# Sliding-window attention and a gated feed-forward network: the RMS root from block 3 on as one GpSimd power, with re-laid orders

## The chip, the core and the metric

The kernel runs on one core of a Trainium2 chip. Its engines are TensorE (PE in the profile; PEld are its weight loads), VectorE (DVE), ScalarE (ACT), GpSimd (POOL) and SyncE (SP). Each works through its own queue in order, and they meet at semaphores. GpSimd and SyncE also issue transfers (DMAs). The metric is the time of one execution on the device, in microseconds (us). Before the change it is 241.68 us, the median of three runs from 241.58 to 241.69.

## What is computed

Attention with a window of 128 keys and 4 sink keys, over 4 batches, 8 heads, 768 positions and head size 64; its output, read as 3072 tokens of 512 numbers, goes through an RMS norm and a gated network of inner size 1536.

```python
def _attn_ref(q, k, v, n_sink, window):
    scores = scale * np.matmul(q, k.transpose(0, 1, 3, 2))
    keep = is_sink | in_window
    scores = np.where(keep, scores, -1000000000.0)
    a = np.exp(scores - np.max(scores, axis=-1, keepdims=True))
    a = a / (np.sum(a, axis=-1, keepdims=True) + 1e-09)
    return np.matmul(a, v)

def _moe_ref(x, w_gate, w_val, w_out, rms_g):
    rms = np.sqrt(np.mean(x * x, axis=-1, keepdims=True) + 1e-06)
    xn = x / rms * rms_g
    g = xn @ w_gate
    silu = g * (1.0 / (1.0 + np.exp(-g)))
    return silu * (xn @ w_val) @ w_out
```

## The kernel before

**Blocks and groups.** The tokens are cut into 24 blocks of 128, numbered g = 0 to 23, six to a batch. Four blocks form a group G = 0 to 5 of the network, 512 tokens wide. Attention of a block needs its own keys and values, those of the block before, and the four sinks. Block g's keys are also met by the queries of block g + 1, so its scores need q of g and g + 1.

**One block's way.** Its q, k and v are loaded in bf16 by GpSimd (`load_bf16`, `load_v`; the transfer converts). q and k are transposed: for g under 8 by TensorE (`pe_t`), with a copy out of the bank by ScalarE or VectorE (`copy_t`, written kT and qT below); from 8 on by a transposing transfer on SyncE's queue (`dma_t`, L459). TensorE makes the scores s (L485, L501, L563), ScalarE their exponentials (L512, L536, L572), VectorE or, from block 16, GpSimd masks them (L547, L584; L526, L597). TensorE multiplies with v in two halves u (`av`, L616, L621), and VectorE divides by the sums (`normal`, n below: L660, L661). Then comes the norm: `square` (L669, ScalarE) sums the squares into `ms`; `rms` (VectorE) makes 1/root of it with six operations on 128 x 1 (L676 adds epsilon, L680 guesses by the number's bits, L689 four times refines) and scales x with it and with the row `gb` (L693, out xr; `gb` holds the norm's weight times the constant `C3` of the refinement). xr is transposed (xt), by TensorE and a copy for g under 8, and by SyncE (`dma_x`, L720) from 8 on.

**The network.** Per group, projections g and v of 12 feature tiles (L975; `ffn`, `mms`), tanh (L982), two VectorE products (L988, p1; L998, h) and the output product (L1008, three parts for each block of 128 tokens), evacuation (L1016, osb) and store (L1020, st). Group 0 is worked in quarters of 128 tokens, groups 1 and 2 in halves, the rest whole.

**The order.** It is written out by hand. Every piece of work is an operation of `plan`, with the ways it can be done, a cost in ns, what it needs and gives, and the PSUM banks it takes and drops. The table `ORDER` lists for each engine the numbers of its operations in order, `TURNS` the sequence in which the engines' lists are taken, `BANKS` the bank for each taking. `Plan.run` follows them, and asserts that all needs have been given. So an engine's queue holds its operations exactly as `ORDER` has them; semaphores come from the data alone. A need such as `("s", g - LOAD_LEAD)` on a load makes no semaphore; it only bounds where the load may stand in the list.

**Names for the lists.** Read with the operations' names, GpSimd's list has, from its 26th place on, and SyncE's from its 8th (q4 is the load of q of block 4; wo0 and wo6 the halves of the output weight; qT, kT, xt the transposes; st0.1 the store of group 0's block 1):

```
GpSimd  q4 v3 k4 q5 q6 wo0 k5 v4 wo6 q7 v8 q8 v5 k6 k7 k8 v6 v7 q9 k9 v9 q10 k10 v10 q11 k11 v11
        q12 k12 v12 ... (in the order of blocks) ... q20, then masks of blocks 16 and 17, k20, ...
SyncE   qT8 qT9 kT8 kT9 qT10 st0.0 qT11 kT10 kT11 qT12 qT13 kT12 kT13 qT14 st0.3 xt8 qT15 xt9 ...
```

Of the kernel before, what the change touches and what calls it, by code (L numbers as in the profile page):

```python
# [96 lines left out]
399 401 400 402 728 418 419 733 420 393 421 409 763 758 778 768 754 773 744 749 427 433
414 783 434-436 448 449 793 450 798 451 442 808 788 819 803 463-466 813 457 824 480 475
482 494 496 497 495 513 488 514 515 504 834 838 516 848 843 853 829 863 868 858 878 873
525 883 531-533 893 509 888 534 899 923 549-551 928 552 938 543 567-569 918 570 585 587  # L100
933 943 948 561 953 579 958 909 904 968 593 963 914 973 1008 1003 994 998 1013 1028 1023
989 1038 1018 1033 984 1053 1048 1043 979 1069 1059 1064 1072 1073
# [29 lines left out]
ASDDSDGDPDPSPDPPPPPGPPPGPDPGPPDDPGAGPPPPADGPPPPGPPSPDPSADPGSDPSPGAAAPAGPAPPDAPPGPPAPDPAP  # L132
PPPADPGPDAGPPDPPDGAPPGPAPPAGDPAPAPDGADAPDGPAPPPADPAGPDAPADAGPPPPAPADGAPADGPPPPPAPPDPGPPD
DPAGPDPAGPDPGAPDDGPDGPDADGDPDGPADADPGAADPGPGDPADGAPDPGADAPGADADPGDPAPPDAPPDADAPGDPPADAGP
AAGPAPDAPPDPADPDAPGDAPDDGDPAPGDPPGSAAPGADAPGDPDGPPPDAGDAPGDADPPGADPAGDSAPPAGASPADPADSADP
PPGADAPGPSADDPGASAPGDPGSAPPGDPSADGAPDASDAPPDADPAGPPSAAADPAADPADPDAPAGADPGADPPDAPPADDPDGS
PDAPASAGDPPAPAGDSPADAPADDPPAGSADPPDASDPAGPADPSDDPGAPDDPADAPDGSDPDGPAGAPADSAPPADSDPPDGPDS
PDAGASPAAPDASGDPADSPDSDPGSPPPDDPSDGPDADPAPADPSDPSPDPSPDDAPDPDAPADPADAPDADAPDPDPASAPDASAP
DSADPADPDPASAPASADPAPPDASDPDAPSDASPADPDADPDPDPDAPASAPPDASADPAGPDGPGDPDGAPDPDPDPDAPAAGPSA
DGPAASGPADSPAGDPPGDDPGPPDGPDAAGPPDAGADPAGPAAGDPADAGPGPDSPGDPDASGPDGAADSPDAPDSDPPDSPDAPDS  # L140
ADPDSAPPDSDPSDAPDASPADDPDPDPADAPAAPDASADPADSPGSDGPDGSPGPGPAPAPADPAPDADPADAPDAGAPDGPGPAAP
AAPPADGDPPDGPDGDGPPAAPDSPGDPGAGPDAPPDPDPDPDAADPADPDDPAPAADPSDPDPDDPAAPPSPDDPAAPDPPSPPDPA
PSDSDSPASDPDPPPAAPDDPDPDPPAAPSDPDPAPDDPDPPPPAAPDADPSDPAAPDPDPAAPDDPDPDAPADPDPDPDPPDPAAPD
# [997 lines left out]
```

## Time and profile before

| | |
|---|---|
| median of three runs | 241.68 us |
| span of the profiled execution, first to last instruction | 241.9 us |
| ScalarE busy | 122.8 us |
| GpSimd busy | 89.2 us |
| loads of q, k, v: issues by GpSimd | 70, 0.89 us each on the mean |

The profile is one execution, taken by the hardware. A row of a group has line, engine, operation, out<-in, count, then after the bar the busy time in us and the mean of one in ns, then the idle time just before and what ended it. A row of a timeline has start and length in us, engine, line, operation, out<-in, count, and in brackets the engine's idle time before it and what ended that. A row of the table by stretches has the stretch, its length, and each engine's busy time with its instructions in brackets (PE, PEld, DVE, ACT, POOL), then the granted clock of TensorE, the busy share of the transfers' engines and GB/s.

### The profile page before, as it was taken

Reading aid. Unit: us, or ns where it says so; the run is one execution under the profiler, and the core shown is the slowest. Engines: PE = TensorE matmul, PEld = TensorE weight load, DVE = VectorE, ACT = ScalarE, POOL = GpSimd, SP = SyncE. Lnnn points to the kernel's source line nnn. Section 1 sums busy time; section 2 is a strip of 40 time slices with the busy share of each in tenths; the row PEclk is TensorE's granted clock in tenths of the full one; section 3 lists DMA queues with packets and bytes.
Section 4 is the critical chain, followed back from the end, with each engine's and each line's share of the span. In section 5 each row is a group of like instructions: output and inputs, shape, how many; then the busy total and the mean of one; then the engine's idle time right before and its main releaser. Section 6 shows DMA issues by size and latency. Waiting matters only on the chain.

```text
span 241.9 us, 5897 instructions
## 1 busy us (share of the span) xinstructions
PE 231.3 (96%) x2329; PEld 147.6 (61%) x2354; DVE 187.4 (77%) x478; ACT 122.8 (51%) x267; POOL 89.2 (37%) x116
## 2 busy tenths in 40 slices
PE   7889999999879999999999999999999999999995
PEld 5568986876668776777876644445554444444443
DVE  3599989989979999999898989994569946537520
ACT  4776368667766574337654464454543321233112
POOL 8985894597526554000004982022540000000000
PEclk9999999999999999999999999999999999999999
DMA  9999999999999999999601999527010114101024
GB/s 128 143 183 195 182 178 194 162 143 139 137 151 152 138 143 154 132 233 156 126 2 24 119 150 123 131 70 128 3 23 0 32 36 173 43 0 47 0 87 173
DMA packets 113741, 27.42 MB, mean 113 GB/s; under 512 B 103857, under 2 KB 110769, under 8 KB 113714
## 3 DMA queue, kind: packets, MB, share of 16 engines
q0 software_dynamic: 81760, 13.90, 79.3%
q1 hardware_dynamic: 31810, 12.95, 29.8%
q8 instruction: 18, 0.29, 0.5%
q10 hardware_dynamic: 144, 0.20, 0.2%
q14 instruction: 9, 0.07, 0.1%
HBM read 28.35 MB, written 6.29 MB: 143 GB/s over the span
## 4 chain that ended last, share of the span: by engine, by line
PE 67%; DMA 20%; POOL 6%; issue 2%; DVE 2%; SPq 2%; POOLq 0%
PE v L975 20%; PE o L1008 20%; PE g L975 18%; DMA wo<-in_moe_w_out_dram 5%; DMA qkT<-q 4%; DMA wv<-in_moe_w_val_dram 4%; DMA wg<-in_moe_w_gate_dram 3%; DMA q<-in_q_dram 3%; POOL v L357 2%; SPq L459 2%; PE s L563 2%; PE av L621 2%; POOL k L353 1%; PE av L616 1%; PE o_last L1028 1%
## 5 line engine op out<-in xcount | busy, mean ns | idle before, releaser
L975 PE MATMUL v<-xnt,wv 128*128 128x128 bf16 (+2 forms) x527 | 72.2, 282 | 0.4 <-DMA wv<-in_moe_w_val_dram 0.2
L975 PE MATMUL g<-xnt,wg 128*128 128x128 bf16 (+2 forms) x521 | 71.3, 281 | 0.4
L1008 PE MATMUL o<-wo,hT 128*128 128x512 bf16 x259 | 65.3, 379 | 1.1 <-issue 0.5
L982 ACT ACTIVATE th<-g 128x512 bf16<-128x512 f32 x72 | 41.7, 599 | 48.4 <-PE g L975 48.2
L988 DVE SCALAR_TENSOR_TENSOR p<-th,g 128x512 bf16<-128x512 bf16 x72 | 48.1, 682 | 18.9 <-ACT th L982 18.7
L975 PEld LDWEIGHTS <-wv 128*128 128x128 bf16 x528 | 43.3, 98 | 21.3 <-DMA wv<-in_moe_w_val_dram 0.6
L998 DVE TENSOR_TENSOR hT<-p,v 128x512 bf16<-128x512 bf16 x72 | 48.1, 682 | 9.3 <-PE v L975 7.8
L975 PEld LDWEIGHTS <-wg 128*128 128x128 bf16 x528 | 42.8, 98 | 19.3 <-issue 1.0
L1008 PEld LDWEIGHTS <-hT 128*128 128x128 bf16 x276 | 25.4, 98 | 26.5 <-issue 0.2
L597 POOL TENSOR_SCALAR_AFFINE_SELECT e<-e 128x512 bf16<-128x512 bf16 x20 | 12.7, 656 | 54.4 <-ACT e L572 53.0
L572 ACT ACTIVATE e<-s 128x384 bf16<-128x384 f32 x52 | 23.1, 495 | 12.5 <-PE s L563 12.5
L1016 ACT ACTIVATE osb<-o 128x512 f32<-128x512 f32 x23 | 13.4, 597 | 21.8 <-PE o L1008 18.0
L357 POOL DMA_DIRECT2D v<-in_v_dram x24 | 21.3, 888 | 8.5 <-DMA q<-in_q_dram 3.8
L353 POOL DMA_DIRECT2D q<-in_q_dram x23 | 20.4, 891 | 9.9 <-DMA k<-in_k_dram 6.7
L353 POOL DMA_DIRECT2D k<-in_k_dram x23 | 20.4, 889 | 9.1 <-DMA v<-in_v_dram 4.5
L669 ACT ACTIVATE sq<-x 128x512 bf16<-128x512 bf16 x24 | 15.1, 631 | 14.8 <-DVE x L661 14.5
L661 DVE TENSOR_TENSOR x<-av,rden 128x256 bf16<-128x256 f32 x48 | 20.4, 424 | 1.7
L693 DVE SCALAR_TENSOR_TENSOR xr<-x,r,gb 128x512 bf16<-128x512 bf16 x24 | 18.7, 778 | 0.8
L621 PE MATMUL av<-v,e 128*128 128x65 bf16 x192 | 16.4, 193 | 0.3 <-DMA v<-in_v_dram 0.3
L536 ACT ACTIVATE e<-s 128x512 bf16<-128x512 f32 (+1 forms) x36 | 15.1, 519 | 1.6 <-PE s L485 1.5
L616 PE MATMUL av<-v,e 128*128 128x65 bf16 x160 | 14.8, 193 | 0.0
L621 PEld LDWEIGHTS <-e 128*128 128x128 bf16 x192 | 12.7, 97 | 2.8 <-DVE e L547 0.4
(78 smaller groups left out, 192.6 us busy)
## 6 DMA issues: line engine op xcount, KB each, us to landing
out_dram<-osb SPq DMA_DIRECT2D x23, 256.0 KB, 2.2
v<-in_v_dram POOLq DMA_DIRECT2D x24, 128.0 KB, 8.9
q<-in_q_dram POOLq DMA_DIRECT2D x23, 128.0 KB, 8.1
k<-in_k_dram POOLq DMA_DIRECT2D x23, 128.0 KB, 9.6
wo<-in_moe_w_out_dram POOLq DMA_DIRECT2D x2, 768.0 KB, 11.3
wg<-in_moe_w_gate_dram POOLq DMA_DIRECT2D x5, 256.0 KB, 8.0
wv<-in_moe_w_val_dram POOLq DMA_DIRECT2D x5, 256.0 KB, 8.9
stage<-in_k_dram SPq DMA_DIRECT2D x1, 256.0 KB, 3.0
```

The source lines that it names most:

```text
L353: nc.gpsimd.dma_start(out=T[name, g], in_=block_of(src, g))
L357: nc.gpsimd.dma_start(out=V16[b][:, t, :, 0:D], in_=block_of(v, g))
L572: nc.scalar.activation(out=e_tile(g)[:, x:x + 2, 0:TW], in_=BANK.pop(("s", g, u, hi))[:, 0:2 * TW].rearrange("p (j c) -> p j c", c=TW), fu ...
L616: nc.tensor.matmul(out=dest, lhsT=T["e", g - 1][:, x, P:2 * P], rhs=V16[b][:, t - 1, h, :], start=(t == 1), stop=False, skip_group_check=True,
L621: nc.tensor.matmul(out=dest, lhsT=T["e", g][:, x, 0:P], rhs=V16[b][:, t, h, :], start=(t == 0), stop=True, skip_group_check=True,)
L661: nc.vector.tensor_tensor(out=T["x16", g][:, 4 * u:4 * u + 4, :], in0=pvv[:, :, 0:D], in1=rden.unsqueeze(2).to_broadcast((P, 4, D)), op=AL ...
L693: nc.vector.scalar_tensor_tensor(out=T["xr", g], in0=T.pop(("x16", g)).rearrange("p h d -> p (h d)"), scalar=r[:, 3:4], in1=gb, op0=ALU.mu ...
L975: nc.tensor.matmul(out=ps[:, i * n:(i + 1) * n], lhsT=w_sb[:, kt, ft * P:(ft + 1) * P], rhs=T["xnt", G][:, kt, cols], start=(kt == 0), sto ...
L982: nc.scalar.activation(out=T["th", key], in_=BANK[("g", key)], func=ACT.Tanh, scale=0.5,)
L988: nc.vector.scalar_tensor_tensor(out=T["p1", key], in0=T.pop(("th", key)), scalar=1.0, in1=BANK.pop(("g", key)), op0=ALU.add, op1=ALU.mult,)
L998: nc.vector.tensor_tensor(out=T[hk][:, i:i + n, cols], in0=T.pop(("p1", key)).rearrange("p (n c) -> p n c", n=n), in1=BANK.pop(("v", key)) ...
L1008: nc.tensor.matmul(out=BANK[("o", G, tb)], lhsT=T["h", G, ft // 4][:, ft % 4, tb * P:(tb + 1) * P], rhs=wo[:, ft, :], start=(ft == 0), sto ...
```

## The change

**The root.** For blocks 0 to 2 `rms` stays on VectorE, with the constant `C3` moved out of `gb` into its own factors. From block 3 (`ROOT_FROM`) the square is taken over 516 columns: x lies in a common tile `xall` with three slots of 512 + 4 columns, and the last four hold constants whose squares bring epsilon into the sum. `root` then is one GpSimd operation on 128 x 1, the power -1/2 of `ms`, and `spread` (VectorE) scales x with it. Three memsets (`eps_columns`) on VectorE prepare the constants.

**Bounds on the lists.** The needs `LOAD_LEAD` and `T_LEAD`, which kept loads and SyncE's transposes behind earlier scores, are gone, as is the need of the scores on the network's progress (`GATE_FROM = NB`). The 16 buffers of q and of k are named one by one (slot g mod 16) instead of being taken in turn.

```diff
-C3 = -5.0 / 16.0
...
-    ld = ctx.enter_context(tc.tile_pool(name="ld", bufs=LD))
+    ld = ctx.enter_context(tc.tile_pool(name="ld", bufs=1))
...
+    xall = const.tile([P, 3, DM + 4], BF16, name="xall")
+    nhalf = const.tile([P, 1], FP32, name="nhalf")
...
+    def eps_columns():
+        for i, c in enumerate((131 * 2.0 ** -13, 139 * 2.0 ** -18)):
+            nc.vector.memset(xall[:, :, DM + 2 * i:DM + 2 * i + 2], c)
+        nc.vector.memset(nhalf, -0.5)
+
+    dve(160, eps_columns, gives=["eps"], prio=-50)
...
-        T[name, g] = ld.tile([P, H, D], BF16, name=name)
+        T[name, g] = ld.tile([P, H, D], BF16, name=name, tag=f"{name}{g % LD}")
...
-            needs = [("s", g - LOAD_LEAD)] if g >= LEAD_FROM else []
+            needs = []
...
-        nc.scalar.mul(gb, BANK.pop(("gb",)), C3)
+        nc.scalar.copy(gb, BANK.pop(("gb",)))
...
-            T["x16", g] = xpool.tile([P, H, D], BF16, name="x16")
+            T["x16", g] = xall[:, g % 3, 0:DM].rearrange("p (h d) -> p h d", h=H)
...
     def square(g):
         T["ms", g] = small.tile([P, 1], FP32, name="ms")
-        sq = xpool.tile([P, DM], BF16, name="sq")
+        n = DM + 4 if g >= ROOT_FROM else DM
+        sq = xpool.tile([P, DM + 4], BF16, name="sq")
         nc.scalar.activation(
-            out=sq, in_=T["x16", g].rearrange("p h d -> p (h d)"), func=ACT.Square,
+            out=sq[:, 0:n], in_=xall[:, g % 3, 0:n], func=ACT.Square,
             scale=1.0 / math.sqrt(DM), accum_out=T["ms", g],
         )
 
+    def root(g):
+        r = T["rs", g] = small.tile([P, 1], FP32, name="rp")
+        nc.gpsimd.tensor_tensor(out=r, in0=T.pop(("ms", g)), in1=nhalf, op=ALU.pow)
+
     def rms(g):
+        if g >= ROOT_FROM:
+            spread(g, T.pop(("rs", g)))
+            return
...
+    def spread(g, r):
         T["xr", g] = xpool.tile([P, DM], BF16, name="xr")
         nc.vector.scalar_tensor_tensor(
-            out=T["xr", g], in0=T.pop(("x16", g)).rearrange("p h d -> p (h d)"),
-            scalar=r[:, 3:4], in1=gb, op0=ALU.mult, op1=ALU.mult,
+            out=T["xr", g], in0=xall[:, g % 3, 0:DM], scalar=r, in1=gb,
+            op0=ALU.mult, op1=ALU.mult,
         )
...
-                   [(n, g)] + old + [("s", g - T_LEAD)], [(n + "T", g)], g,
+                   [(n, g)] + old, [(n + "T", g)], g,
...
+        if g >= ROOT_FROM:
+            pool(570, lambda g=g: root(g), [("ms", g)], [("rs", g)], early, mode=9)
-        dve(1745, lambda g=g: rms(g),
-            [("ms", g), "gb"] + ([("xt", g - 3)] if g >= 3 else [])
+        dve(700 if g >= ROOT_FROM else 1745, lambda g=g: rms(g),
+            [("rs" if g >= ROOT_FROM else "ms", g), "gb"] + ([("xt", g - 3)] if g >= 3 else [])
```

**The orders.** All five lists, `TURNS` and `BANKS` are new. Read by names, the lists agree with the old ones up to TensorE's 85th operation, ScalarE's 34th, GpSimd's 25th and SyncE's 8th, and on VectorE, the new memsets left out, up to its 33rd. TensorE has the same 375 operations in another order; from its 298th place on (the end of group 3's output for its third block) the order is the old one. Six copies out of banks go from ScalarE to VectorE (kT of blocks 3, 4, 5 and 7, xt of 4 and 6). GpSimd's and SyncE's lists become (rs is the root, e16.0 a mask of block 16):

```
GpSimd  q4 k4 k5 q5 v3 wo0 v4 wo6 q6 rs3 v5 q8 k6 q7 k7 rs4 v6 q9 k8 k11 q10 rs5 v7 q11 k9 rs6
        k10 v8 rs7 v10 q15 v9 q17 v11 k12 k15 q13 k14 k16 q12 rs8 v12 k13 q14 rs9 q16 rs10 v13
        rs11 q20 k18 rs12 v15 k19 q18 k17 v14 v16 q19 rs13 k22 rs14 v18 e16.0 v17 e16.1 v20 v23
        e16.2 q22 e16.3 rs15 e17.1 e17.0 v22 k21 v19 k23 k20 rs16 q21 rs17 e19.0 ...
SyncE   qT8 kT8 qT9 st0.1 qT10 qT11 kT9 st0.0 kT11 kT10 qT13 qT12 xt9 kT12 xt8 kT14 kT13 st1.0
        qT15 st0.3 qT14 qT16 qT17 xt10 xt11 kT15 st0.2 kT17 st1.1 qT20 kT16 kT18 st1.2 qT18 ...
```

On TensorE, ahead of the scores of block 8 the new list has the projection g of group 1's tiles 4 and 5 and the sink scores of batch 1 more and the transpose of x of block 6 less; ahead of the scores of block 9 two further projections v of group 1; between the scores of block 13 and the attention of block 14 stand four output parts, eight projections, the scores of blocks 14 and 15 and the attention of block 13. ScalarE has the square of block 12 right behind the four exponentials of block 13.

More of the change, by code (lines that the diff above doesn't have):

```diff
@@ L97 @@
[L97 to L102, printed above, removed]
+25 21 23 200 178 176 179 177 183 181 182 184 169 189 223 205-207 212 208 213 210 192 211
@@ new lines @@
+218 227 229 228 230 196 620 221 237 625 640 635 650 630 655 262 645 246 248 247 249 281
+266-269 256 285 198 660 287 670 665 275 299 293 301 686 675 325 303 305 304 306 297 691
+329-332 700 313 705 710 681 715 338 346 696 347 720 348 321 349 362 725 363 342 364 365
+730 355 735 761 378-380 323 740 381 371 745 394 755 750 396 409 387 410 411 790 412 785
+402 780 766 800 429-432 419 776 445 425 795 446-448 805 815 771 461 462 820 438 830 463
+464 454 810 477-480 841 825 835 470 495 497 510-513 489 846 851 530-532 503 865 533 860
@@ L122 @@
-518 519 535 538 537 536 110 553 555 554 571 573 556 572 588 586 574
+26 9 10 27-29 32 35 31 33 38 36 30 39 34 40 42 43 41 44 46 48 45 49 47 50 51 55 54 37 53
+52 57 58 257 56 61 59 64 65 276 60 67 62 74 70 294 66 73 68 314 71 63 339 72 85 69 91 75
+77 86 79 83 89 76 356 78 80 82 372 88 388 81 403 100 95 420 87 98 94 92 84 90 97 439 107
+455 96 481 93 482 102 111 483 106 484 471 498 496 108 104 99 110 101 490 103 504 534-536
+105 537 521 109 543 553 556 554 555 572 574 573 591-593 575 562 609 607 594 581 600 615
@@ L131 @@
 TURNS = """
[L132 to L143, printed above, removed]
@@ L144 @@
-SPSDPPPPPAAPSASSPAADS
+ASDDDDSPGPPDDPPPSPPPPPGPPGPDPGDDPDSGASGASPPPPGDSPPPPPPPDGPADDPGPPAAGAPAAPPPGADPPPPAPDPGAPPPPDAPPDGAPPDPG
+PDAPGPPAPPGAADGPADPAPDGPDAPPAPGDAPPADPAGPADAPPPGPPAAADGPADGPPPPPAPPDPGPPDDPAGPDPAGPDGPDPGDDPDGPAAGPDGDPD
+GPAGPDAGDPDAPPDADAPDPDPADADPAPAPADPDPDAPDADPAPDPAPDAPAGAGDAPAGPPDPGDPDGDPDGDPAADPASDPGDPPGADPGDDPGPDPDPG
+APGAPAGDPAGDPDPAGDSPDGPADSAPADPASDSAPDAPPAPAPDADPASADPAAGPDGSPDAGDAPPDSASPDPDDPAPDPAGADSGPADGPDPAGADAPDA
+GDPDGPAGPDAGADPPPDGAPADGPADDGPAAGDPAGPDGDPSGPAGPAPPDADPAAAPPASDDAPDGPGDPDSDPAPDASAPADSAPDPDSPDPDPSDDPDSD
@@ new lines @@
+SPPAPDSASDPAGAGPAPSDADPSDPPADADPPAGDAGPDSDGPDPDADPDPADAPDSAPDAADSPAGGPASAGPAPPADGAPDGAADPGDPDGPAGDPDPADS
+PDSPSPAPPDASDPADASPDGDPGSASPDADPASADPAGPSAGDAPDASDPAADGPSGASPAGDPSGPDGPDPDGPDGDPPGDADPGDPASAPPGASPGAAGDP
+PADGDPGDAPDGPPDGPDAAGPPDGPAAPAAPAGPADAGPDASGAPDAGDSPGDPGPDSPDGAPDGSDSAPDPDSDPDASPDDPADPSDAPDASDAPDGPSDPD
+SPADSDPDPASAPAAPDAADPGDGPADGPDGPDPPAAPAPDAPAPDAGPDAGDPGDPPAAPPAPDADPAAPAPGDDPGDGPGPAGAPPDGDPSGDAGPADSPPD
+PDPDDPAADPAGDPDDPADGSPADAPDDPDPSPAAPPPDDPAAGPDPSPPPDPASPDSDSPASDPDPPPAADPDPDPDPPAASPDPDPADPDPDPPPPAADPAD
@@ L152 @@
+4062431047356204362147352061752046712406436035430543205643250463725706423154720165241307
+6254625173406251703246157043620715361205712457130257143065375143207165420654376124357604
+5361725425361732610432610453705642173056421057342153067213041672503160732516326535032701
+6542734047025320731430545620367540627546
 """
@@ L199 @@
     PE_MASKS = 2
+    ROOT_FROM = 3
     TRI_FROM = 4
@@ L204 @@
     LD = 16
-    GATE_FROM = 8
-    LOAD_LEAD = 10
-    LEAD_FROM = 10
+    GATE_FROM = NB
     WARM = 56
     GATE_LEAD = 14
-    T_LEAD = 4
     SPLIT = (0,1)
@@ L954 @@
             dve(600, lambda b=b: sink_k(b),
-                [("kT", g), ("s", g + 1)] + ([("ss", b - 2, i) for i in ((2, 4) if b - 2 < 2 else (2,))]
+                [("kT", g)] + ([("ss", b - 2, i) for i in ((2, 4) if b - 2 < 2 else (2,))]
                                if b >= 2 else []), [("ksk", b)], 0.1 * g)
```

36 lines of the change are left out of this document (16 added, 20 removed), and 69 rows, old and new, of the table ORDER.

## The prediction, as it went on record before the change was run

> **What bounds the kernel now.** The page first: its span and its first part.
>
> ```profile
> span 241.9 us, 5897 instructions
> ...
> PE 231.3 (96%) x2329; PEld 147.6 (61%) x2354; DVE 187.4 (77%) x478; ACT 122.8 (51%) x267; POOL 89.2 (37%) x116
> ```
>
> TensorE works 96% of the span. The question is therefore not how much work VectorE loses, but which of TensorE's idle microseconds the change can reach. The table by stretches says where they lie (second number: length; third: PE busy).
>
> ```profile
> 0.00:22.00 22.00, 18.75 (x242) 13.39 (x243) 14.52 (x54) 14.38 (x35) 18.43 (x28) 1.00 1.55 159
> 22.00:60.00 38.00, 37.16 (x571) 30.43 (x573) 34.06 (x85) 24.73 (x53) 27.50 (x32) 1.00 2.09 170
> 60.00:72.00 12.00, 9.89 (x140) 7.52 (x138) 10.28 (x28) 8.20 (x19) 5.53 (x7) 1.00 1.97 138
> 72.00:126.00 54.00, 53.58 (x621) 40.34 (x627) 50.75 (x131) 30.29 (x67) 13.11 (x15) 1.00 1.47 140
> 126.00:239.00 113.00, 111.97 (x770) 55.95 (x779) 77.49 (x183) 45.22 (x97) 24.58 (x35) 1.00 0.43 71
> ```
>
> Idle is length minus busy: 3.25 us before 22 us (the prologue, whose orders the change keeps), 0.84 from 22 to 60, 2.11 from 60 to 72, 0.42 and 1.03 in the 167 us behind, and the 2.9 us tail after 239. VectorE is 94% busy from 72 to 126 (50.75 of 54), yet TensorE waits 0.42 us there: VectorE is full but holds nobody up. The clock column is 1.00 throughout. The list of waits names the 2.11:
>
> ```profile
> PE s L563 <- DMA qkT<-q: 1.3, 1, 1.3
> ...
> PE s L563 <- DMA qkT<-k: 0.8, 1, 0.8
> ...
> PE av L621 <- DMA v<-in_v_dram: 0.3, 1, 0.3
> ```
>
> The timelines of TensorE and of SyncE's queue (two answers) show which:
>
> ```profile
> 65.68 0.54 PE L563 MATMUL s<-qkT 64*64 64x192 bf16 x24 [0.78 <-DMA qkT<-k]
> 70.49 0.54 PE L563 MATMUL s<-qkT 64*64 64x192 bf16 x24 [1.32 <-DMA qkT<-q]
> ```
> ```profile
> 47.82 7.97 SPq L459 DMA_TRANSPOSE qkT<-q  x2
> 55.88 3.77 SPq L459 DMA_TRANSPOSE qkT<-k  x2
> 59.75 1.29 SPq L459 DMA_TRANSPOSE qkT<-q  x1
> ```
>
> These are the scores of blocks 8 and 9. By SyncE's old order (q8, q9, k8, k9, q10) k8's transpose goes out at 55.88 and its scores start 9.8 us later; q10's at 59.75 and its scores start 10.7 us later. So the kernel is TensorE's work plus two waits on transposes that went out late and then took long: 0.78 + 1.32 = 2.10 us. That is nearly all there is to win.
>
> **The change, part by part.** *The root.* One block's root as it is (VectorE, then ScalarE before it; block 3):
>
> ```profile
> 37.33 0.18 DVE L660 RECIPROCAL rden<-av 128x4 f32<-128x4 f32 x1
> 37.55 0.42 DVE L661 TENSOR_TENSOR x<-av,rden 128x256 bf16<-128x256 f32 x1
> ...
> 39.28 0.15 DVE L676 TENSOR_SCALAR m<-ms 128x1 f32<-128x1 f32 x1
> ...
> 40.57 0.75 DVE L693 SCALAR_TENSOR_TENSOR xr<-x,r,gb 128x512 bf16<-128x512 bf16 x1
> ```
> ```profile
> 38.04 0.63 ACT L669 ACTIVATE sq<-x 128x512 bf16<-128x512 bf16 x1
> 38.57 0.19 ACT L669 ACTIVATION_READ_ACCUMULATOR sq<-x 128x1 f32 x1
> 38.76 1.64 ACT L572 ACTIVATE e<-s 128x384 bf16<-128x384 f32 x4
> ```
>
> From m to xr, 40.57 - 39.28 = 1.29 us of VectorE go, 21 times (blocks 3 to 23): 27.1 us. Back come six bank copies that move from ScalarE to VectorE (k's transposes of blocks 3, 4, 5, 7, x's of 4 and 6), 0.42 each by the rows below: 2.5 us, and three memsets in the prologue. VectorE ends near 163 us. On the path this is worth nothing, since TensorE did not wait for VectorE. What hides it is TensorE's own work; were that shorter, up to 24 us would count. Four columns more in the square are lost in its 0.63 us.
>
> ```profile
> L452 ACT COPY qkT<-k 128x512 bf16<-128x512 bf16 x5 | 2.9, 584 | 2.8 <-PE k L445 2.8
> L452 DVE COPY qkT<-k 128x512 bf16<-128x512 bf16 x3 | 1.3, 419 | 1.6 <-PE k L445 1.6
> L597 POOL TENSOR_SCALAR_AFFINE_SELECT e<-e x20: 624/651/852, 126.6 to 179.5; 128x512 bf16<-128x512 bf16 x20
> L693 DVE SCALAR_TENSOR_TENSOR xr<-x,r,gb x24: 750/752/1136, 13.1 to 195.1; 128x512 bf16<-128x512 bf16 x24
> ```
>
> *The power's price* is not in this trace. From below: m, a 128x1 operation, 0.15 us. From above: a select of 512 columns held up by a VectorE operation, 0.65 + 1.14 = 1.8. The plan charges the select 590 + 60 ns, and the row has 651; it charges the power 570 + 60. I take 0.63 as an estimate, nearest to the select. With a handoff on both sides (0.07 from x to the square above, say 0.1) the root is 0.83, less than the 1.29 it replaces.
>
> *What the root does to GpSimd's queue* is the dangerous part. GpSimd issues the q, k and v loads, 0.89 us each:
>
> ```profile
> L353 POOL DMA_DIRECT2D k<-in_k_dram x23 | 20.4, 889 | 9.1 <-DMA v<-in_v_dram 4.5
> ```
>
> Until now they ran far ahead; now loads stand behind a root, the root waits for its block's square, and so the loads wait for the attention. Two stretches of the DMA view (kind of load or transpose, last number: median us from issue to landing; first 46 to 100, then 108 to 160) show what a load and a transpose cost when many are under way and when few are:
>
> ```profile
> k<-in_k_dram POOLq DMA_DIRECT2D x11, 128.0 KB, 13.2
> ...
> qkT<-k SPq DMA_TRANSPOSE x8, 9.4
> ```
> ```profile
> k<-in_k_dram POOLq DMA_DIRECT2D x4, 128.0 KB, 5.2
> ...
> qkT<-k SPq DMA_TRANSPOSE x6, 2.4
> ```
>
> A load costs 5.2 to 13.2, a transpose 2.4 to 9.4. Since roots let only a few loads out at a time (five behind root 4, three behind root 5, two behind root 6), I count nearer the low ends.
>
> *Scores 8 and 9.* TensorE was free for them at 65.68 - 0.78 = 64.90 and 70.49 - 1.32 = 69.17. The new order puts one projection group (0.87 us, below) more ahead of scores 8, and trades a transpose group for a sink group of like size; ahead of scores 9 two more: they are wanted at 65.8 and 69.17 - 0.78 + 1.74 = 70.1.
>
> ```profile
> 92.28 0.47 PE s L563 x16
> ...
> 98.06 0.26 PE av L621 x8
> 98.32 0.86 PE o L1008 x4
> 99.18 0.87 PE v L975 x8
> ```
> ```profile
> 45.92 0.18 ACT L669 ACTIVATION_READ_ACCUMULATOR sq<-x 128x1 f32 x1
> ```
> ```profile
> 52.24 0.20 ACT L669 ACTIVATION_READ_ACCUMULATOR sq<-x 128x1 f32 x1
> ```
>
> k8 now stands behind root 4, v6 and q9. Square 4 ended at 46.1; with its later place on ScalarE say 46.7, root to 47.5, two issues of 0.89, k8 out at 49.3, landed at 54.5; its transpose, now ahead of q9's, lands 2.4 to 9.4 later, 57 to 64. In time for 65.8. k9 stands behind root 5 (square 5 ended at 52.4, root to 53.2), v7 and q11: out at 55.0, landed 60.2, transposed 62.6 to 69.6. In time for 70.1. If both are slow, k8's scores come 5.4 us late or more; the bounds are thus a gain of 2.10 and a loss of several us. I take the gain: **-2.10**. The 0.32 us wait for v (block 5) I leave as it is: v5 now goes out behind root 3, but the large output weight ahead of it sets its landing.
>
> *New tight places.* (a) The transpose of x of block 3 stands three output groups, the scores of block 5 and a sink group behind its attention: 3 x 0.86 + about 0.5 = 3.1 us of cover. The chain is 0.1 + 0.64 (L660 and L661) + 0.79 (to the square's end) + 0.1 + 0.63 + 0.1 + 0.75 + 0.1 = 3.2: **+0.1**; between 0 and 1.3 by the power's bounds. (b) v14 stands behind root 12 and four loads, and ScalarE has square 12 behind the exponentials of block 13. From the end of scores 13 to the first half of attention 14 the new order has 12 projection and output groups (12 x 0.87 = 10.4 us), two score groups (1.0) and two of attention (0.5): 11.9. The chain: 0.2, exponentials 1.64, 0.1, square 0.72, root 0.83, four issues 3.6: 7.1; landing 5.2: 7.1 + 5.2 - 11.9 = **+0.4**; 0 to 8.4. k17 stands in the same queue, with k16's transpose behind k17's on SyncE: the same wait, not a second. (c) Shorter leads elsewhere (scores to attention of block 6 fall from 3.8 to 2.8 us of TensorE work, of block 17 from 5.0 to 3.6, with root 15 just ahead of mask 17 on GpSimd): **+0.3**, an estimate, 0 to 2. Behind such a root stand masks, and attention waits for those. All other moves (outputs, SyncE's stores, banks) keep TensorE's work the same and have leads of 10 us or more.
>
> The sum: -2.10 + 0.1 + 0.4 + 0.3 = -1.3. The profiled span of 241.9 lies 0.2 above the median of the runs, 241.68; taken from the median: **240.4 us**.
>
> **Rivals.** *Loads late behind the roots (slower).* If v14 lands not in 5.2 but halfway to 13.2, in 9.2 us, attention 14 waits 7.1 + 9.2 - 11.9 = 4.4, and the sum is -2.1 + 0.1 + 4.4 + 0.3: 244.4. It decides for slower from a landing of 6.5. For it: the 13.2 is this kernel's own. Against: most loads are then done, and the row of 5.2 has stores and transposes beside it too.
>
> *The power is dear (slower).* At 1.8 us, 1.17 more, (a) is 1.3, (b) 1.6, (c) say 0.5: -2.1 + 3.4 = +1.3, 243.0; from about 1.3 it is no gain. For it: VectorE's two-input operations and GpSimd disturb each other; xr takes 0.75 alone and 1.14 at its worst, under a select of the masks:
>
> ```profile
> 132.72 1.14 DVE L693 SCALAR_TENSOR_TENSOR xr<-x,r,gb 128x512 bf16<-128x512 bf16 x1
> ```
> ```profile
> 132.69 0.63 POOL L526 TENSOR_SCALAR_AFFINE_SELECT e<-e 128x512 bf16<-128x512 bf16 x1 [3.48 <-ACT e L512]
> ```
>
> The Trainium skill, "SBUF — State Buffer", section "Who interferes with whom", says that a VectorE instruction with two SBUF inputs and a GpSimd instruction that reads SBUF shut each other out for a whole instruction; the trace agrees (0.39 us added). By it a root may wait out a mask of VectorE, and the price would be nearer this rival's. Against it: half of VectorE's operations here read one input from PSUM.
>
> *One wait stays (same).* If k9's transpose takes 9.4 and its load 6.6, scores 9 come near 71 and wait about as before: -0.78 + 0.7: 241.6.
>
> *The first power costs a pause (same).* The one load of an engine's tables or code that this trace shows as an instruction is ScalarE's:
>
> ```profile
> L349 ACT ACT_TABLE_LOAD x1 | 1.3, 1283 | 0.8 <-PEq L1122 0.8
> ```
>
> Such a 1.28 us at root 3 would come on top of (a), which has no cover left: 240.4 + 1.28 = 241.7. Against it: GpSimd's first select, of the same trace, shows none. The Trainium skill, "GPSIMD Engine Reference", section "Instruction dispatch", tells of about 6 us at the first call of freshly loaded code, which would make it some 246; no run here shows it.
>
> **From these to the numbers.** Forecast 0.56, late loads 0.16, the dear power 0.13, the one wait that stays 0.12, the pause 0.03. A measurement here tells 0.2% (0.5 us) from nothing. Faster is the forecast, 0.56; same 0.12 + 0.03 = 0.15; slower 0.16 + 0.13 = 0.29. The forecast's own range is 239.1 (tight places nothing, the 0.3 us of v5 and part of the 0.84 us before 60 gone too) to 241.2. The whole range goes to 243.4: it holds the dear power and the lesser half of the late loads; outside are the other half, 0.08, the dearest powers, 0.04, and some 0.04 below.
>
> **What would show it.** Right: scores 8 and 9 start without a DMA wait in TensorE's timeline; loads of 55 to 110 us land in 5 to 7 us; power rows near 0.63; VectorE near 163 us; PE idle between 60 and 72 under 0.4. Wrong: waits of attention on v or of scores on qkT between 90 and 125 (late loads); power rows over 1.3, or TensorE waiting at the transpose of x (dear power); GpSimd idle for long on a root with VectorE behind it, or any new wait that I have not named that sums to over 1.4 us.

## The result, and the profile after

The changed kernel takes 240.57 us (median of five runs, 240.55 to 240.69). The kernel before, in five runs beside it, takes 241.69 (241.58 to 242.11). The ratio is 0.9945, with a 95% interval of 0.9929 to 0.9961: 1.1 us faster.

The first lines of the page after:

```profile
span 239.0 us, 5806 instructions
...
PE 231.5 (97%) x2328; PEld 148.6 (62%) x2354; DVE 167.1 (70%) x361; ACT 118.8 (50%) x261; POOL 104.2 (44%) x137
```

TensorE has as much work as before (231.5 against 231.3). VectorE has lost 20.3 us, and GpSimd has gained 15.0. The page lists 2328 matmuls and 2354 weight loads: some matmul records are missing from this trace, as from those of before, a0 and e4 to e9 (2328 or 2329); the other traces have all 2354. Idle time of some 0.4 us in a long stretch, with no wait to go with it, can be such missing records. The table by stretches, to be read as that of before (stretch, length, busy time of PE, PEld, DVE, ACT, POOL, then TensorE's clock):

```profile
0.00:22.00 22.00, 19.22 (x239) 14.12 (x240) 13.90 (x57) 14.12 (x35) 18.25 (x28) 1.00 1.56 159
22.00:60.00 38.00, 37.66 (x582) 31.38 (x584) 30.98 (x70) 21.79 (x47) 22.19 (x27) 1.00 1.79 163
60.00:72.00 12.00, 11.95 (x157) 9.11 (x156) 11.28 (x22) 7.59 (x19) 8.54 (x11) 1.00 1.34 151
72.00:126.00 54.00, 53.47 (x630) 40.63 (x636) 44.08 (x90) 30.48 (x69) 27.40 (x34) 1.00 1.43 140
126.00:236.00 110.00, 109.20 (x733) 53.38 (x744) 66.52 (x125) 44.85 (x94) 27.79 (x40) 1.00 0.48 74
```

TensorE's idle time from 60 to 72 us has fallen from 2.11 to 0.05. Of the rest, 0.47 went in the prologue (3.25 to 2.78), whose orders are the same, and 0.50 from 22 to 60 (0.84 to 0.34). Neither can be put down to the change: the kernel before, profiled once more (e0 below), has 2.74 and 0.10 there. Behind 72 us nothing is won: 0.53 idle up to 126, where it was 0.42. The timelines of SyncE's queue and of TensorE (start, length, operation) show the two places at which the kernel before waited:

```profile
47.52 1.30 SPq L465 DMA_TRANSPOSE qkT<-q  x1
53.59 2.00 SPq L465 DMA_TRANSPOSE qkT<-k  x1
55.69 1.21 SPq L465 DMA_TRANSPOSE qkT<-q  x1
57.00 0.53 SPq L1039 DMA_DIRECT2D out_dram<-osb  x1
57.63 2.54 SPq L465 DMA_TRANSPOSE qkT<-q  x2
60.26 1.22 SPq L465 DMA_TRANSPOSE qkT<-k  x1
```
```profile
65.31 0.54 PE L569 MATMUL s<-qkT 64*64 64x192 bf16 x24
...
69.61 0.54 PE L569 MATMUL s<-qkT 64*64 64x192 bf16 x24
```

kT8 now stands ahead of qT9; the scores of blocks 8 and 9 start with no wait (no bracket in the row). The view of transfers, 46 to 100 us, shows in its last number that loads and transposes take little more than a third of what they took (13.2 and 9.4 us before):

```profile
k<-in_k_dram POOLq DMA_DIRECT2D x11, 128.0 KB, 4.6
...
qkT<-k SPq DMA_TRANSPOSE x7, 3.8
```

**A profile is one execution.** In every later run with a profile, an execution's time lies 1.67 to 1.85 us over its span (the changed kernel's profiled one: 240.69 and 239.0). By that, the profile of before, with a span of 241.9, shows an execution of about 243.6 us (an estimate), just above the highest that the kernel before ran in the experiments (240.8 to 243.4), and not its median. Its span stood 2.9 above that of after; the medians differ by 1.1. So a typical execution before holds less waiting than the 2.10 us that its profile shows, and the next profile of it, e0 below, holds one wait in place of two.

### The profile page after: what moved, and what is told of

Its sections match the earlier page's. It is cut to its first block, busy times and chain, and to the rows that moved or that the text cites. A ratio compares the mean times of both kernels' runs of the same rounds, so it can differ in the third digit from the quotient of the medians.

```text
span 239.0 us, 5806 instructions
## 1 busy us (share of the span) xinstructions
PE 231.5 (97%) x2328; PEld 148.6 (62%) x2354; DVE 167.1 (70%) x361; ACT 118.8 (50%) x261; POOL 104.2 (44%) x137
## 4 chain that ended last, share of the span: by engine, by line
PE 89%; POOL 4%; DMA 3%; issue 1%; ACT 1%; DVE 0%; POOLq 0%
PE v L994 26%; PE g L994 26%; PE o L1027 25%; DMA wv<-in_moe_w_val_dram 3%; PE s L569 3%; PE av L627 2%; PE av L622 2%; PE o_last L1047 1%; POOL k L359 1%; ACT e L542 1%; POOL q L359 1%; PE s L491 1%; PE x L725 1%; POOL v L363 1%; PE av L612 1%
## 5 line engine op out<-in xcount | busy, mean ns | idle before, releaser
L1001 ACT ACTIVATE th<-g 128x512 bf16<-128x512 f32 x72 | 41.9, 599 | 53.6 <-PE g L994 51.4
L1017 DVE TENSOR_TENSOR hT<-p,v 128x512 bf16<-128x512 bf16 x72 | 48.6, 684 | 11.2 <-PE v L994 10.2
L994 PEld LDWEIGHTS <-wv 128*128 128x128 bf16 x528 | 42.9, 98 | 20.3 <-issue 0.8
L683 POOL TENSOR_TENSOR rp<-ms,nhalf 128x1 f32<-128x1 f32 x21 | 13.4, 640 | 62.7 <-ACT sq L676 62.7
L676 ACT ACTIVATE sq<-xall 128x516 bf16<-128x516 bf16 (+1 forms) x24 | 15.2, 634 | 15.9 <-DVE xall L667 12.0
L1035 ACT ACTIVATE osb<-o 128x512 f32<-128x512 f32 x23 | 13.5, 603 | 19.0 <-PE o L1027 15.7
L363 POOL DMA_DIRECT2D v<-in_v_dram x24 | 21.9, 913 | 0.6 <-DMA wv<-in_moe_w_val_dram 0.4
L603 POOL TENSOR_SCALAR_AFFINE_SELECT e<-e 128x512 bf16<-128x512 bf16 x20 | 14.0, 717 | 17.5 <-ACT e L578 16.9
L666 DVE RECIPROCAL rden<-av 128x4 f32<-128x4 f32 x48 | 8.7, 180 | 18.4 <-PE av L627 18.3
L667 DVE TENSOR_TENSOR xall<-av,rden 128x256 bf16<-128x256 f32 x48 | 20.4, 425 | 1.7
L359 POOL DMA_DIRECT2D q<-in_q_dram x23 | 21.1, 918 | 1.0 <-POOLq L1141 0.8
L710 DVE SCALAR_TENSOR_TENSOR xr<-xall,rp,gb 128x512 bf16<-128x512 bf16 x21 | 16.3, 780 | 3.2 <-POOL rp L683 3.2
L627 PE MATMUL av<-v,e 128*128 128x65 bf16 x192 | 16.7, 193 | 0.0
```

What stands on the lines that cost most here:

```text
L359: nc.gpsimd.dma_start(out=T[name, g], in_=block_of(src, g))
L363: nc.gpsimd.dma_start(out=V16[b][:, t, :, 0:D], in_=block_of(v, g))
L627: nc.tensor.matmul(out=dest, lhsT=T["e", g][:, x, 0:P], rhs=V16[b][:, t, h, :], start=(t == 0), stop=True, skip_group_check=True,)
L667: nc.vector.tensor_tensor(out=T["x16", g][:, 4 * u:4 * u + 4, :], in0=pvv[:, :, 0:D], in1=rden.unsqueeze(2).to_broadcast((P, 4, D)), op=AL ...
L710: nc.vector.scalar_tensor_tensor(out=T["xr", g], in0=xall[:, g % 3, 0:DM], scalar=r, in1=gb, op0=ALU.mult, op1=ALU.mult,)
L994: nc.tensor.matmul(out=ps[:, i * n:(i + 1) * n], lhsT=w_sb[:, kt, ft * P:(ft + 1) * P], rhs=T["xnt", G][:, kt, cols], start=(kt == 0), sto ...
```

## The experiments

Theory A: the powers hold GpSimd's loads back, so that fewer are under way, transposes are quick, and the waits before scores 8 and 9 go. Theory B: it is the relief of VectorE. A third, C, came up on the way: only kT8's time of landing counts, however it is reached. Idle columns are TensorE's idle microseconds by the tables of stretches; the 0.42 from 72 to 126 us is that of traces with missing records (in e4 the list of waits has none there).

| run | what it is | ratio to before (95%) | idle 22 to 60 | 60 to 72 | 72 to 126 |
|---|---|---|---|---|---|
| e0 | before, again | 0.9997 (0.9975 to 1.002) | 0.10 | 1.66 | 0.00 |
| e1 | root alone, old lists | 0.997 (0.9951 to 0.999) | 0.53 | 0.00 | 0.00 |
| e2 | e1, new loads and transposes | 1.0069 (1.0039 to 1.0099) | 1.81 | 0.60 | 0.00 |
| e3 | after, loads as in e1 | 1.0081 (1.0051 to 1.011) | 0.66 | 0.00 | 0.48 |
| a0 | after, again | 0.9973 (0.9958 to 0.9987) | 0.35 | 0.05 | 0.53 |
| e5 | old lists, powers as gates only | 0.9958 (0.9943 to 0.9974) | 0.32 | 0.00 | 0.42 |
| e6 | old lists, VectorE relieved only | 0.9956 (0.9941 to 0.9971) | 0.60 | 0.00 | 0.42 |
| e8 | after, no power | 1.0167 (1.0141 to 1.0193) | 0.50 | 0.05 | 2.92 |
| e4 | before, one exchange on SyncE | 0.9977 (0.9963 to 0.9991) | 0.85 | 0.00 | 0.42 |
| e7 | after, root on VectorE | 1.0647 (1.0623 to 1.067) | 2.33 | 0.60 | 3.55 |
| e9 | after, each power twice | 1.0059 (1.0032 to 1.0086) | 0.98 | 0.05 | 0.75 |
| e10 | e1 with two exchanges | 1.0002 (0.9984 to 1.0021) | 1.70 | 0.00 | 0.00 |

**e0: the kernel before once more.**

> The kernel before, unchanged, once more with a profile of its own. The changed kernel's span is 1.6 to 1.7 us below its time (239.0 for 240.69), while the profile of before had a span of 241.9 for a median time of 241.68. If that profile stands for the runs, the span is again near 241.9, with waits of 0.8 and 1.3 us before the scores of blocks 8 and 9. If it was one dear execution, the span is near 240.0 (241.7 less 1.7) and the two waits sum to about 0.2 us or other idle time is missing; then the change's gain of 1.1 us needs another account than those waits alone.

241.77 us. TensorE's timeline has one wait, not two; behind its row stand those of SyncE's queue:

```profile
65.84 0.54 PE L563 MATMUL s<-qkT 64*64 64x192 bf16 x24 [1.66 <-DMA qkT<-k]
```
```profile
46.87 9.98 SPq L459 DMA_TRANSPOSE qkT<-q  x2
56.95 2.52 SPq L459 DMA_TRANSPOSE qkT<-k  x2
```

kT8, at 56.95, is the third in SyncE's list. qT9 ahead of it left only at 54.59, when the load of q9 had landed, and k8 had lain there since 51.3 (issued at 40.87, 10.4 to its landing). kT8 then took 8.8 us and landed 1.6 us after TensorE was free for its scores. This execution too is dearer than the median, 242.36 against 241.77, so a usual one waits less than 1.66.

**e1: the root alone.** The code of the change, all lists as before, the powers put in among GpSimd's loads.

```diff
 GpSimd, by names
-q8 v5 k6 k7 k8 v6 v7 q9 k9 v9 q10 k10 v10 q11 ...
+q8 v5 rs3 k6 k7 k8 v6 rs4 v7 q9 k9 v9 q10 k10 v10 rs5 q11 ...
```

> The changed code with the orders of before on all engines; the GpSimd powers are put into the old GpSimd list at the places where the squares ended in the old profile, so the loads still run far ahead. VectorE loses about 27 us, nothing else moves. Theory A (TensorE waits for transposes, not for VectorE): waits of 0.8 and 1.3 us before the scores of blocks 8 and 9 remain, time within 0.4 us of before, 241.3 to 242.1. Theory B (the gain is the work taken from VectorE): 240.6 or less.

240.93 us: between what the two theories said, and most of the whole change's gain without any of its new lists. The wait before scores 8 is gone, and one for v5, which the first profile of before had too (0.32), is 0.53 long here; its row in TensorE's timeline:

```profile
49.05 0.19 PE L626 MATMUL av<-v,e 128*128 128x65 bf16 x1 [0.53 <-DMA v<-in_v_dram]
```

**e2: the new order of loads and transposes under TensorE's old order.** Lists of GpSimd up to root 7 and of SyncE up to kT10 from the change, all else as e1.

```diff
 GpSimd
-q4 v3 k4 q5 q6 wo0 k5 v4 wo6 q7 v8 q8 v5 rs3 k6 ...
+q4 k4 k5 q5 v3 wo0 v4 wo6 q6 rs3 v5 q8 k6 q7 k7 rs4 ...
```

> As the one with the root alone, but GpSimd's list up to root 7 and SyncE's list up to the transpose of k of block 10 are the new ones (store 0.0 for 0.1); TensorE, VectorE and ScalarE keep the old order. Theory A: fewer loads are under way between 46 and 66 us, transposes of blocks 8 and 9 land in 2.5 to 5 us, both waits go, 240.3 to 240.9 if no load behind becomes late. Theory C (what counts is that the new TensorE order wants scores 8 and 9 later, by 0.9 and 1.7 us): part of the waits stays, 241.0 to 241.6.

243.2 us, slower than either theory said, though transposes are nearly as quick as after the change (4.4 and 4.7 us from 46 to 66 us, where that has 4.2). The load of q7 now stands behind root 3, v5, q8 and k6; it goes out at 41.65 and lands 6.0 later, and TensorE's old order wants it early:

```profile
47.72 0.40 PE L450 MATMUL q<-ident,q 128*128 128x128 bf16 x4 [1.79 <-DMA q<-in_q_dram]
```

The scores of block 9 wait too, 0.60 us, for a kT9 that left at 62.9 by the new list. So quick transposes alone win nothing; an order of loads serves only the order of TensorE that it was made for.

**e3: the new order with the loads of e1.** The changed kernel; behind q6 GpSimd's loads and roots stand as in e1, and the last eleven loads between the masks of block 17 and root 16.

```diff
 GpSimd
-q6 rs3 v5 q8 k6 q7 k7 rs4 v6 q9 k8 ...
+q6 q7 v8 q8 v5 rs3 k6 k7 k8 v6 rs4 v7 q9 k9 ...
```

> The changed kernel with its orders, but from the load of q of block 6 on the loads stand in the old order and run ahead of the roots as in the kernel before (roots where squares ended in the old profile). Theory A: the transposes take 8 to 10 us again between 48 and 70 us; scores 9 wait up to 1.5 us, and the time is 0.5 to 1.5 us above the changed kernel, 241.1 to 242.1. Theory C (the later place of scores 8 and 9 on TensorE suffices): 240.4 to 240.9.

243.77 us, slower than either theory said. There is no wait before scores 8 or 9, although the transposes took 6.3 and 7.3 us. What is lost lies elsewhere; of the 3 us in the span (242.0 against 239.0), 0.83 are at masks of GpSimd, with those eleven loads ahead of them in its list:

```profile
145.62 0.20 PE L626 MATMUL av<-v,e 128*128 128x65 bf16 x1 [0.48 <-POOL e L602]
...
146.21 0.20 PE L626 MATMUL av<-v,e 128*128 128x65 bf16 x1 [0.35 <-POOL e L602]
```

That placing was this experiment's own, so it does not settle what earlier loads cost.

**a0, e5, e6, e8: gates and relief apart.**

> The changed kernel unaltered, to stand beside the three others on one chip. Both theories: 0.993 to 0.997 of before, no wait of 0.3 us or more before the scores of blocks 8 and 9.

240.57 to 241.84, median 241.01: the changed kernel's gain is 0.27% here (0.66 us), where it was 0.55% (1.12 us) at first. The two intervals barely touch, and why the first five runs did better is open; the chips may differ.

```diff
 e5, in rms: the six operations for every block
-        if g >= ROOT_FROM:
-            spread(g, T.pop(("rs", g)))
-            return
-            out=m, in0=T.pop(("ms", g)), scalar1=1e-6, scalar2=-10.24, op0=ALU.add, op1=ALU.mult,
+            out=m, in0=T.pop(("ms", g)), scalar1=0.0 if g >= ROOT_FROM else 1e-6, scalar2=-10.24,
+            op0=ALU.add, op1=ALU.mult,
 e5, in root: issued, the result unused
-        nc.gpsimd.tensor_tensor(out=r, in0=T.pop(("ms", g)), in1=nhalf, op=ALU.pow)
+        nc.gpsimd.tensor_tensor(out=r, in0=T["ms", g], in1=nhalf, op=ALU.pow)
 e6 (on e1) and e8 (on the changed kernel), root: no instruction
-        r = T["rs", g] = small.tile([P, 1], FP32, name="rp")
-        nc.gpsimd.tensor_tensor(out=r, in0=T.pop(("ms", g)), in1=nhalf, op=ALU.pow)
+        T["rs", g] = T.pop(("ms", g))
```

> The lists of the root alone (e1), with the powers still issued on GpSimd at their places, so that GpSimd's loads stand behind them, but their results unused: VectorE computes the root with its six operations for every block. Theory A (what the root alone won, ratio 0.997 and no wait before the scores of blocks 8 and 9, comes from the powers holding GpSimd's loads back, so that fewer are under way and the transposes are quick): 0.996 to 0.998, no wait before scores 8 and 9, and transposes of blocks 8 and 9 shorter than the 8.4 us of before. Theory B (it comes from the 27 us taken off VectorE): 0.999 to 1.002, with VectorE near 193 us.

> The lists of the root alone, with no power at all: VectorE scales x by the mean square itself, so from block 3 on the root is left out of the computation. VectorE is relieved as in e1 and GpSimd's loads stand behind nothing new. Theory A: 0.999 to 1.002, with a wait of 1 to 2 us before the scores of block 8 and transposes of 8 us. Theory B: 0.994 to 0.998, without needing the transposes to be quicker.

Each theory holds of one of the two runs and fails of the other: gates alone win 0.42%, relief alone 0.44%, and either is as good as both together (e1) or as the whole change. The two have one thing in common. In SyncE's timelines the first kT8 goes out 2.3 us earlier than in e0 in the one and 1.6 in the other (first e5, then e6):

```profile
46.77 7.74 SPq L464 DMA_TRANSPOSE qkT<-q  x2
54.61 3.35 SPq L464 DMA_TRANSPOSE qkT<-k  x2
```
```profile
47.27 7.97 SPq L464 DMA_TRANSPOSE qkT<-q  x2
55.34 3.11 SPq L464 DMA_TRANSPOSE qkT<-k  x2
```

q9's load, for which qT9 and behind it kT8 wait, took 5.5 us in e5, 7.2 in e6 and 8.3 in e0; kT8 landed at 62.6 and 63.9, where e0 had 65.8. In e6 the transposes are as slow as in e0 (kT8 8.6 us): quick transposes were not needed. But e6's kT8 had little to spare: its scores start at 64.40, 0.5 us after the landing. Why the relief alone brings q9's load in earlier is not settled; e0's profile is of another chip, and in the two profiles of the kernel before alone kT8 goes out a microsecond apart (55.88 and 56.95).

> The changed kernel with all its orders, without the powers: x is scaled by the mean square itself, so from block 3 on the root is left out of the computation. GpSimd's loads leave as soon as the buffers allow. Theory A (the powers' hold on the loads is what makes the new order work): the loads of 46 to 66 us take 8 us or more again, qT8 and kT8 too, and scores 8 or 9 wait; ratio 0.998 to 1.006. Theory B (relief of VectorE, and the order of the lists): loads without the hold leave earlier and land in time, ratio 0.990 to 0.996, at or below the changed kernel's own.

245.7 us, beyond theory A's range. Its mechanism holds (without the powers' hold the loads are slow and a transpose comes late), but not its place: scores 8 and 9 did not wait. The price lies further on. SyncE issues the transposes ahead of scores 12 at the same times as in the changed kernel (kT12 at 85.41; a transpose of x that waits for its xr stands ahead of it), but 13 loads issued from 72 to 90 us take 7.6 to 7.9 us each, in the changed kernel nine and 4.6 to 4.7, and kT12 lands late (TensorE of e8, then of the changed kernel):

```profile
93.01 0.61 PE L491 MATMUL s<-qkT 64*128 64x256 bf16 x8 [1.72 <-DMA qkT<-k]
```
```profile
90.84 0.61 PE L491 MATMUL s<-qkT 64*128 64x256 bf16 x8
```

**e4, e7, e9: kT8 alone, the relief and the price in the new order.**

```diff
 e4, SyncE's list of the kernel before
-qT8 qT9 kT8 kT9 qT10 ...
+qT8 kT8 qT9 kT9 qT10 ...
 e7: the changed kernel with the two edits of e5
 e9, in root
+        nc.gpsimd.tensor_tensor(out=r, in0=T["ms", g], in1=nhalf, op=ALU.pow)
         nc.gpsimd.tensor_tensor(out=r, in0=T.pop(("ms", g)), in1=nhalf, op=ALU.pow)
```

> The kernel before with one exchange in SyncE's list: qT8 kT8 qT9 kT9 in place of qT8 qT9 kT8 kT9; the root stays on VectorE and all else is as before. Theory C (all that was won is the one wait before the scores of block 8, because kT8 stands in SyncE's queue behind qT9, which waits for the load of q of block 9 that lands near 54.6 us, while k of block 8 has landed near 51.3 us): kT8 leaves near 51.4 us and lands by 61 us, no wait of 0.3 us before the scores of block 8, ratio 0.993 to 0.997. Theory A (the number of loads under way sets how long the transposes take, so without holding loads back nothing is won): the wait moves to the scores of block 9, 0.998 to 1.001.

Two names exchanged in one list: 241.01 us, the median of a0. The ratio, 0.9977, falls between the two theories' ranges; it is near that of a0 (0.9973) and short of the first measurement of the change (0.9945). Theory C's step came as it said, with loads slower than in e0 (k 11.8 us from 46 to 66, where e0 had 10.3 at most) and transposes as slow (8.2). SyncE, and TensorE at scores 8:

```profile
47.10 1.50 SPq L457 DMA_TRANSPOSE qkT<-q  x1
50.72 1.20 SPq L457 DMA_TRANSPOSE qkT<-k  x1
54.15 1.19 SPq L457 DMA_TRANSPOSE qkT<-q  x1
```
```profile
64.36 0.55 PE L561 MATMUL s<-qkT 64*64 64x192 bf16 x24
```

kT8 leaves at 50.72, takes 8.7 and has landed 4.9 us before its scores start. Behind it there is nothing more to win: from the 17th tanh to the end of the span it is 171.2 us in e0 (240.6 - 69.4) and 171.3 in e4 (239.2 - 67.9). ScalarE's rows for that tanh in e0 and e4:

```profile
69.37 0.60 ACT L982 ACTIVATE th<-g 128x512 bf16<-128x512 f32 x1 [0.33 <-PE g L975]
```
```profile
67.89 0.60 ACT L980 ACTIVATE th<-g 128x512 bf16<-128x512 f32 x1 [0.33 <-PE g L973]
```

> The changed kernel with all its orders and with the powers still issued, so that the loads stand behind them as in the change, but their results unused: VectorE computes the root with its six operations for every block. Theory C (VectorE's relief is worth nothing, only the transposes' time of landing counts): 0.993 to 0.998, no different from the changed kernel, VectorE near 193 us. Rival B (the new order leans on the relief): 0.999 to 1.004, with waits of TensorE for VectorE's x, xr or transposes' copies from block 3 on.

257.25 us: the rival holds, and far beyond its numbers. The new order cannot do without the relief. VectorE is busy 190.0 us of a 254.8 span, a share of 75%, and it was 77% in the kernel before, where, behind the prologue, its list of waits has no matmul that waited for VectorE. So the share does not tell it; the place in the order does. In the waits, and in the two timelines at 88 us (VectorE, TensorE), the product h stands behind a root:

```profile
PE s L569 <- DVE hT L1015: 2.1, 2, 1.9
PE x L723 <- DVE xr L708: 1.9, 3, 0.8
PE v L992 <- DVE p L1005: 1.5, 2, 1.3
```
```profile
87.87 0.15 DVE L687 TENSOR_SCALAR m<-ms 128x1 f32<-128x1 f32 x1
...
89.17 0.75 DVE L708 SCALAR_TENSOR_TENSOR xr<-xall,r,gb 128x512 bf16<-128x512 bf16 x1
89.84 1.28 DVE L1015 TENSOR_TENSOR hT<-p,v 128x512 bf16<-128x512 bf16 x2
```
```profile
90.57 0.60 PE L992 MATMUL g<-xnt,wg 128*128 128x256 bf16 x4 [1.08 <-DVE hT L1015]
```

The next projection waits for h, whose end frees a bank; h stands behind 1.97 us (87.87 to 89.84) of the six operations and xr. These waits are not the whole price: in e7, too, TensorE's clock falls behind a pause (the last section).

> The changed kernel with each of the 21 powers issued twice. GpSimd busy near 118 us. Theory C: the power's price is not on the path; each load is held 0.64 us longer and still lands in time: 0.993 to 0.998. Rival (the price of the power runs through the loads and the masks into the end): 0.998 to 1.005, with new waits of TensorE for a transpose or for v.

242.77 us: the rival holds, and a little beyond its range. 0.0086 in ratio against a0 is 2.1 us for 13.1 us more of GpSimd (104.2 to 117.3). The first of it can be seen at root 3 (GpSimd, then TensorE at the transpose of x of block 3):

```profile
40.67 0.91 POOL L683 TENSOR_TENSOR rp<-ms,nhalf 128x1 f32<-128x1 f32 x1 [7.79 <-ACT sq L676]
41.65 0.55 POOL L684 TENSOR_TENSOR rp<-ms,nhalf 128x1 f32<-128x1 f32 x1
```
```profile
43.05 0.40 PE L726 MATMUL x<-ident,xr 128*128 128x128 bf16 x4 [0.65 <-DVE xr L711]
```

**e10: a version meant to join the gains.** e1 with the exchange of e4, and v5 a place earlier against the wait that e1 had:

```diff
 SyncE
-qT8 qT9 kT8 kT9
+qT8 kT8 qT9 kT9
 GpSimd
-v8 q8 v5 rs3
+v8 v5 q8 rs3
```

> The root alone in the old lists (e1), with two exchanges: kT8 ahead of qT9 on SyncE, and the load of v of block 5 ahead of that of q of block 8 on GpSimd. Theory C (the wait before the scores of block 8 is all there is to win, and from 69 us on TensorE is the bound in any of these orders, at 171.2 us to the end): no wait of 0.3 us from 22 us on, neither for kT8 nor for v, ratio 0.993 to 0.997, as the changed kernel and no better. Rival (held loads, a relieved VectorE and the early transpose add up): ratio under 0.992.

241.76 us, a miss of both. v5 and kT8 came in time, and there is no wait before scores 8. But q8, one place later, took 13.5 us to land, at 49.2; qT8 left then, and block 7's scores, which meet the queries of block 8, waited for it (SyncE, TensorE; the profiled execution, 242.67 us, is 0.9 dearer than the median, so the usual wait is shorter):

```profile
49.20 1.30 SPq L464 DMA_TRANSPOSE qkT<-q  x1
```
```profile
56.37 0.54 PE L568 MATMUL s<-qkT 64*64 64x192 bf16 x24 [1.60 <-DMA qkT<-q]
```

Theory C's statement that kT8 is all there is to win is thus too narrow: it is whichever of qT8, kT8 and v5 lands last against TensorE's need. In the old order each of the three came late in one profile or another: by 1.60 (e10), 1.66 (e0) and 0.53 us (e1). No run here is clearly better than the changed kernel.

## Why the prediction was right

The time was right to 0.2 us against the first measurement and to 0.6 against a0 (241.01). That it was so near was in part luck: the sum came out by two terms that were too large in opposite senses, 2.10 for the waits and 0.8 for new tight places.

- **TensorE's waits are all there is to win: right.** From 72 us on neither the change nor any experiment gained anything.
- **"-2.10" for the waits before scores 8 and 9: the place right, the size too large.** Both went. But the sum was read from a profile and then taken off the median, with the remark that the span lies 0.2 above it. A time lies 1.7 above its span, so that profile was of an execution of about 243.6 us. Between medians the change is worth 1.1, in a0 0.7.
- **The times of k8 and k9: right.** k8 was to go out at 49.3 and land at 54.5: 49.6 and 53.6. Its transpose was to land between 57 and 64: 59.2. k9 was to go out at 55.0 and land at 60.2: 54.5 and 60.1.
- **Roots let fewer loads out, so transposes are quick: so it is, and it was not what the gain needs.** e4 wins as much as a0 with transposes of 8 us. What the gain needs is that kT8 lands before TensorE wants it: in e4 because it no longer stands behind q9's load, in e5 and e6 because that load lands sooner. In the changed kernel kT8 lands at 59.2 and is wanted at 65.3; with the transposes slow again (e3, e8) its scores still don't wait, and no run there takes only kT8's place away. For the new lists, though, the quick transposes are a condition (e8).
- **The relief of VectorE is worth nothing on the path: right of the changed kernel's time only in that nobody waited for VectorE before.** The working named the cover, and that "up to 24 us would count" without it. The new order uses that cover up: without the relief it loses 16 us (e7, 257.25 against 241.01 in a0). That a re-laid order would spend the slack was not seen. And in the old order the relief alone won as much as the whole change (e6). VectorE was to end near 163 us busy and has 167.1: the 1.29 us from m to xr that the working takes off 21 times hold gaps between the operations, which were never busy time (in e7's rows of block 3 some 0.15 of 1.30 us, which over 21 blocks makes 3 of the 4 us).
- **The power at 0.63: right on the mean, 0.64.** The rows of it, and of the xr behind:

```profile
L683 POOL TENSOR_TENSOR rp<-ms,nhalf x21: 547/563/1105, 40.8 to 190.9; 128x1 f32<-128x1 f32 x21
...
  POOL rp L683: 3.2, 5
```

The median is 0.56, so the mean is made by a few dear ones, below; xr waited for a root five times, 3.2 us in all, and no matmul for any of them. The rival that charged the power 1.17 us more had it at 2.6 us in the time; e9 charged 0.64 more and lost 2.1. Its mechanism exists (a dearer power does reach the time); only the price was not there.
- **New tight places, +0.1 +0.4 +0.3: too dear, 0 in the trace.** TensorE's row for the transpose of x of block 3 has no wait; v14 goes out at 107.2 and lands at 112.5 with no wait of attention 14 for it; nor is there one of TensorE for a mask. Since e9 turns the first into 0.65 us, that cover was nearly used up, as the working had it.
- **v5's wait stays: wrong, by 0.32 us to the good.** It went out later than before (41.7 against 36.0) and landed earlier (45.9 against 48.9). But e0, the kernel before, has no such wait either, so this is not shown to be the change's.
- **"5.4 us late or more" if load and transpose of k8 are both slow:** by its own terms 49.3 + 13.2 + 9.4 - 65.8 = 6.1. Nothing else hangs on it.
- **The rivals.** Late loads: none waited for in this kernel (e8 shows what they cost). The one wait that stays: not in the trace. The pause at the first power: its row is 0.91 us long, under a mask of VectorE, and no pause of its own is to be seen.

## What to carry to other kernels

Before a gain is read out of one profile, set its span against the median of the times: a wait seen in a dear execution may be half as large in a usual one. Here times lay some 1.7 us over spans. Where a transfer lands on the edge of its need, look first at what stands ahead of it in its queue: here one exchange of two names won 0.23%, and a new root and five new lists 0.27% to 0.55%. A re-laid order spends the slack that the change gives it, and so becomes dependent on it: ask what it costs to lose each of the reliefs it was laid for.
